# Loading one batch of queries in rows of two tokens, with the list of jobs ordered anew

## The chip, the cores and the metric

The kernel runs on one core of one Trainium2 chip. The metric is device time in microseconds (us): before the change the median of three runs is 262.52 us (262.32 to 262.54). A core has five engines that work side by side and wait for each other through semaphores: TensorE (PE, with the loading of its weights shown as PEld), VectorE (DVE), ScalarE (ACT), GpSimd (POOL) and SyncE (SP), which here only issues transfers. ACT issues a few transfers too.

## The reference, cut to what matters

Two blocks follow each other. The first is a linear attention over polynomial features; the second is a mixture of four attention experts, of which each token takes two.

```
def phi(x):                                  # 64 features of each token
    a = einsum('rd,bhsd->bhsr', S1, x); b = einsum('rd,bhsd->bhsr', S2, x)
    return einsum('bhsi,bhsj->bhsij', a, b).reshape(..., 64)
kv, z = einsum('bhsf,bhsd->bhfd', phi(k), v), sum(phi(k), over s)
x = (phi(q) @ kv) / (phi(q) @ z + 1e-6)      # (4, 4, 1088, 32) -> (4, 1088, 128)

logits = x @ w_gate;  the two best of 4 experts for each token, with softmax weights w
for e in range(4):
    a = softmax(causal((x @ wq[e]) @ (x @ wk[e]).T / 8))
    out += w_e * (a @ (x @ wv[e]) @ wo[e])   # only for tokens that chose e
```

Batch 4, heads 4, sequence 1088, head size 32, model size 128, all in float32.

## The kernel before, in words

The kernel is a list of 1284 small **jobs** (class `Plan`, L73). A job has a name, the engines it may run on, what it reads and makes, and a function that emits its instructions. `ORDER` (L21) is a list of job numbers, found ahead of time; a letter behind a number picks the first or second of the engines that the job may use. The program emits the jobs in that order. Each engine then works through its own jobs strictly in the order of the list, and waits where an input isn't there. So the list fixes the order on PE, DVE, ACT, POOL and SP, and also which of the four PSUM buffers ("pair0" to "pair3") a job gets.

Work goes by batch, and each batch in two halves. `prepare` (L423) computes x of the first block and the choice of experts; `queries`, `scores` and `values`/`outputs` (L1059 to L1324) do the experts' attention in 17 tiles of 64 tokens, in three groups (tiles 0 to 5, 6 to 11, 12 to 16). The preparation of batch b+1 lies between the attention jobs of batch b. Batch 0 has nothing in front of it; its preparation is the start-up of the kernel and uses a path of its own (`early`):

- `load k0` (L428), `load q0` (L435, `by_head`, four transfers of one head each, two issued by SP and two by ACT), `load v0` (L439, four transfers on SP). k's rows in memory are 2 KB and more, v's about 1 KB. For q, partition 32h + t holds tokens t, t + 32, t + 64 and so on of head h: each piece that a transfer moves is one token, 32 numbers or 128 bytes.
- `turn k`, `turn q` (DVE, L484 and L494) transpose 32x32 blocks, `project` (PE, L562) multiplies by both sketches at once, `low` (copy, L570) and `lift` (L574) add the high and low part, `multiply` (L580) forms the 64 features. For k they are multiply k0.0, k0.1, k0+.0, k0+.1; for q multiply q0.0 and q0+.0, .1, .2.
- `spread v0`, `spread v1` (L451) put v into place; `sums 0.0`, `sums 0.1` (PE, L619) form kv and z.
- `turn qf` (PE, L666) transposes q's features in four pieces of 6, 4, 4 and 4 blocks of 128; `keep qf` (L668) copies them out of PSUM; `numer` (L692), `divide` (L699 to L701) and `turn x` (L707) give x and its transpose, `keep x` copies that.
- `logits` (L884), `turn logits` (L888), `choose a`/`choose b` (L911 to L927) choose the experts. `store masks` and `fetch masks` (L990, L1003) send the choices through memory to all partitions; `query` (L1066), `base` and `pick` (L1079) form each token's queries for its two experts; `score` (L1104), `take` (L1116), `exp` (L1132), `guard`, `invert`, `weigh` (L1147), `turn A` (L1152), `sum` (L1180), `out` (L1251, L1277, L1301) follow.

`turn w0` to `turn w2` (L390) transpose the experts' weights, `dummy` jobs (L250) are matmuls on zeros that nobody reads. L193 is the line of a copy helper that many jobs share. Jobs of features and joins for batches 1 to 3 (`features`, L537) run mostly on POOL.

Tokens stand in their natural order from the features on. In q's path the order comes from the load:

```
eng.dma_start(out=dst[32 * h : 32 * h + 32, 0:S].rearrange("p (c d) -> p c d", d=D),
              in_=src[b, h].rearrange("(c t) d -> t c d", t=32))
```

Column block c of partition t is token 32c + t, so after a 32x32 transpose the columns are tokens in order.

Of the kernel before, what the change touches and what calls it, by code (L numbers as in the profile page):

```python
# [21 lines left out]
0 1 2 3 4 78 79 83 15a 80 45 21a 48 46 10a 81 90 53b 52b 91 54b 50 25b 18a 49 55b 5b 12a 14a 51 82 84 87 85 86 94 64  # L22
63 95b 96 27a 57 56 58 92 99 93 98b 100a 65 104 97a 101 400 89b 66a 108 103a 88a 105a 114 68 69 106 102b 70 109a 401
115 71a 110 116a 117a 107a 113a 402 399 118 124 111a 112a 59 60 120 61 406 119a 410 125a 122 405 121a 126 67 403 409
127 413 123a 414 128 408 415 134 129a 130 62 407 135 154 131 72 74 73 75 417a 419a 132 155 77 133a 136 404 137a 412
160 161 418a 140 187 138 162 163 156 158 170 188 76 157 693 192a 159 171 175 47 164 165a 176 692 191a 416a 166 189
167a 178 190 691 145 421 177 420 193 141 694 194 411 195 196 197 179 216 230 209 217 182 172 701 422a 183 218 231 198a
424 423 425 428a 223 139 219a 202 173 232 210 233a 427b 184 199 220 174a 221 180 426b 211 702 429 224 203 234 253 222
212b 254 213 185 258a 326 41b 257a 181 431 144 39b 225 255 204 235 186a 256 153 28b 236 430 200 214 226b 215 432 327
149 143 330a 331a 259 205a 142 227 329 700 438 228 168 260 433 148 332 201 328 268 698 229 206 169a 276 434 275 24b  # L30
439 207 283 699 333 277 284 208 269 261 435a 278 270 300 299 285 262 286 436a 287a 237 440 696 279b 442a 437 301 238
9b 705 695 280 441a 288 263 443 264a 708 706 302 152 281 239 303b 240a 271b 241a 289 242a 272 444 709a 282 265 304 245
244 445a 290 704 359 358 712a 273 351 446a 274 350 305 306 707a 266 147 243a 292 710a 366 713a 360 291 367 26b 267 352
361 293 369 362a 11b 353 342 343 38b 294 711a 987 246 697 151 368 363 370 464 295a 296 297 344 345 714 715 371 298 465
447 466 30b 33b 716b 146 354b 467 985 469 364 307 308 247 346b 450 309 310 717 372a 373 718 355 703 311 19b 721a 374
365 448 722b 988 470 312 719 375 468 316a 313b 720b 315b 335 314a 317 480 334 479 474 318 356 475 336 357 320 319 471
723 483a 481 337 484a 476 482 347 449 724 338b 485 486 339 451 348 340 322 321 508 725 509 487 323 548 472 501 349 488
547 324a 515 341 502 516 993 726 732 510 489 545 986 494 727 546 503 495 376 496 150 490b 477 478a 517 511a 994 733
377 995 728 518a 491 991 378 549a 504a 512 379 454 380 730b 492 729b 734 493 550b 497a 551 519 989 731 452 522 381 552
736b 382 735a 383 737 513 455 384 505 498 523 453 592 514 388a 591 385b 506 499 250 386a 249 996 524 463 461 525b 387a  # L40
593 560 526 390 248 16b 389 500 992 594 251a 738 527 595a 568 520 561 325 521 507 567 740a 391 739a 528 569 570 576
392 562 575 571b 596 563a 553 999 473 577 554 597 1002 564 462 758 621 555 458 572 759 620 1000 619 618 760 556b 578
990 573 529 579a 623a 761 530 531 534a 557 622b 558 598 624 583 1001a 580 625 584 559 393 585 651 459 532b 763 535a
1005a 1003a 764 565 581 457 533a 650 1004a 762 536 537 586 574 394 659 582 566 1007a 587a 652 658 539 643 634 538 653
635 660 661 588 589 662 642 1006a 774 773 398 460 778a 777a 590 627 644 636 645 654b 456 663 626 664b 646a 637 655 765
628 665 779 776 666 775 629 768 1008 780 1009 599 741 1010a 667 1012 630a 769 997 631 743 396 647 656 638a 600 632 657
1016a 1011 31b 601 252 639 602 633 603 742 604 1013 541 648 608a 606a 998 607b 640 605b 609 1015b 610 542 816 540 611
1014a 649 612 543a 817 795 809 766 745 641 744 810 811 770 796 812b 1017 668 771 1019 1026 544 669 670 1027 671 788
1018 749 672 748 797 1020 798a 818 673 674 751 819a 789 675 676 781 1021 678a 679a 772a 1028 1022 820 1023a 1024b 813
799 790 1025 756 1029b 1030a 814 682 782 815 791b 677a 615 681 614 680b 821 783 792 800 839 840 842 793 802 841 1031  # L50
683 843a 844a 845 613 803 1032 794 846 804 616a 757 805a 806 877 878 684 869 870 1034b 784b 912 1033a 913 755 807 746
747 917a 822 879 871 880 801 785 1052 767 1053 861 916a 786 787 872 862 808 886 1054 873b 918 885 874 881b 887 854 855
888 847 856 915 848 882 875 914 1055 889a 876 857b 883 858 849 617 13b 863 1057 823 850a 884 824 919 890 859 851 891
864 852 825 860 395 829b 826a 685 830 827b 865a 828a 944 936 1056 831 1062 686 945 921 892 920 1063 833 937 946 832
397 953 947 948b 853 922 1139 1138 952 866 1142a 867 938 955 949 1058 954 956 1143a 834 32b 1060 1140 1141 836 939 835
# [1335 lines left out]
```

## Time and profile before

| | |
|---|---|
| median of the runs shown | 262.52 us |
| the profiled execution's own time | 263.49 us |
| its span, first to last instruction | 261.8 us |
| PE busy | 254.9 us (97%) |
| DVE busy | 208.4 us (80%) |
| POOL busy | 157.5 us (60%) |
| ACT busy | 105.6 us (40%) |
| granted TensorE clock | 0.999 |

The span is what the profile's times count from; 1.7 us of the profiled execution lie around it. "Busy" for PE is an upper bound, since matmuls are pipelined and their ends are modelled. In a row of the timeline the first number is the start, the second the duration, both in us; "x" counts the instructions merged into the row, and square brackets tell how long the engine idled before and what released it. In the chain of waits the two numbers are start and length.

### The profile page before, as it was taken

How to read it: one execution, taken by the hardware profiler on the slowest of the kernel's cores; microseconds unless marked ns; L12 is line 12 of the kernel's file. 1: busy time of each engine (PE TensorE's matmuls, PEld its weight loads, DVE VectorE, ACT ScalarE, POOL GpSimd, SP SyncE). 2: the span in 40 equal slices, each digit the busy share in tenths (PEclk: the TensorE clock that was granted, in tenths of full speed). 3: DMA queues.
4: the chain of work that ended last, by engine and by line, in shares of the span. 5: the costliest groups of instructions: out<-in, count | busy, mean ns of one | idle time of the engine just before them, and what ended most of it. 6: DMA issues, size and time to landing. Idle time of an engine off the chain costs nothing.

```text
span 261.8 us, 9228 instructions
## 1 busy us (share of the span) xinstructions
PE 254.9 (97%) x3811; PEld 192.2 (73%) x3811; DVE 208.4 (80%) x529; ACT 105.6 (40%) x279; POOL 157.5 (60%) x266
## 2 busy tenths in 40 slices
PE   7899999999999999999999999999999999999995
PEld 2787666646958887665897986666689875589994
DVE  5778999999998996998887497998994388893442
ACT  3453354757242225532814044635514215723120
POOL 5546776899578716597467682366273842542642
PEclk9999999999999999999999999999999999999999
DMA  7978689891467275906044685003370379240012
GB/s 149 212 122 186 112 207 168 158 146 20 73 135 166 67 184 114 148 4 183 3 84 83 143 167 120 4 3 90 93 120 4 96 141 238 47 96 3 5 30 59
DMA packets 87739, 27.35 MB, mean 104 GB/s; under 512 B 58576, under 2 KB 87056, under 8 KB 87696
## 3 DMA queue, kind: packets, MB, share of 16 engines
q1 hardware_dynamic: 85184, 26.15, 50.7%
q10 hardware_dynamic: 2512, 0.61, 1.0%
q8 instruction: 30, 0.49, 0.8%
q14 instruction: 13, 0.11, 0.2%
HBM read 22.22 MB, written 4.52 MB: 102 GB/s over the span
## 4 chain that ended last, share of the span: by engine, by line
PE 84%; DMA 8%; DVE 5%; POOL 1%; issue 1%; SPq 0%; ACT 0%; DVEq 0%; POOLq 0%; ACTq 0%
PE pair L1180 28%; PE pair L1104 24%; PE pair L1066 9%; PE pair L1301 7%; DMA mb<-md 4%; PE pair L1251 3%; PE pair L523 2%; PE pair L827 2%; DMA in<-in_q_dram 2%; DMA w<-in_v_dram 2%; PE pair L627 2%; DVE w L1116 1%; PE pair L1277 1%; DVE fp L805 1%; PE pair L619 1%; PE pair L692 1%
## 5 line engine op out<-in xcount | busy, mean ns | idle before, releaser
L1147 POOL TENSOR_SCALAR w<-w,rs,sh 128x256 f32<-128x256 f32 (+14 forms) x68 | 56.8, 840 | 34.4 <-DVE rs L1143 32.8
L1104 PE MATMUL pair<-xT,qs 128*128 128x320 f32 (+9 forms) x216 | 74.0, 478 | 0.4 <-DVE qs L1079 0.4
L1132 ACT ACTIVATE w<-w,mx 128x64 f32<-128x64 f32 (+15 forms) x68 | 52.4, 772 | 45.8 <-DVE mx L1116 40.6
L1116 DVE CUSTOM_DVE_ANT_0 w<-pair,mask 128x64 f32<-128x64 f32 (+14 forms) x68 | 48.3, 723 | 15.4 <-PE pair L1104 13.0
L1104 PEld LDWEIGHTS pair<-xT,qs 128*128 128x128 f32 x216 | 38.8, 190 | 25.9 <-issue 11.1
L1152 DVE STREAM_TRANSPOSE AT<-w 128x320 f32<-128x320 f32 (+15 forms) x68 | 51.2, 762 | 3.4 <-POOL w L1147 3.0
L1180 PEld LDWEIGHTS pair<-AT,xra 32*128 32x128 f32 x1136 | 41.6, 185 | 4.6 <-issue 2.0
L1180 PE MATMUL pair<-AT,xra 32*128 32x160 f32 (+5 forms) x1136 | 44.9, 303 | 0.0
L1207 POOL TENSOR_TENSOR agg<-agg,mb 128x768 f32<-128x768 f32 (+1 forms) x22 | 34.0, 1559 | 3.4 <-DVE agg L1203 2.0
L1066 PE MATMUL pair<-xT,Mq 128*128 128x384 f32 (+1 forms) x96 | 34.0, 475 | 0.0
L193 ACT COPY agg<-pair 128x384 f32<-128x384 f32 (+1 forms) x31 | 13.2, 463 | 45.5 <-PE pair L1180 44.0
L1180 PEld LDWEIGHTS pair<-AT,xrb 32*128 32x128 f32 x752 | 26.4, 185 | 2.4 <-issue 2.2
L1180 PE MATMUL pair<-AT,xrb 32*128 32x160 f32 (+5 forms) x752 | 28.0, 289 | 0.0
L1140 POOL TENSOR_SCALAR rs<-zs 128x1 f32<-128x1 f32 x32 | 6.8, 214 | 34.0 <-ACT w L1132 23.5
L1066 PEld LDWEIGHTS pair<-xT,Mq 128*128 128x128 f32 x96 | 17.3, 190 | 10.3 <-issue 3.2
L1079 DVE COPY_PREDICATED qs<-mb,pair 128x768 f32<-128x768 uint16 (+1 forms) x24 | 23.1, 962 | 1.5 <-ACT qs L193 0.3
L537 POOL TENSOR_TENSOR fp<-w 128x576 f32<-128x576 f32 x19 | 22.6, 1209 | 1.6 <-DVE w L527 1.1
L1301 PEld LDWEIGHTS pair<-Mo,agg 128*128 128x128 f32 x168 | 20.6, 192 | 2.4 <-issue 0.5
L1301 PE MATMUL pair<-Mo,agg 128*128 128x128 f32 x168 | 21.4, 277 | 0.0
L193 ACT COPY qs<-pair 128x384 f32<-128x384 f32 (+1 forms) x21 | 9.2, 463 | 19.5 <-PE pair L1066 14.2
L1203 DVE COPY_PREDICATED agg<-mb,pair 128x384 f32<-128x384 uint16 (+1 forms) x24 | 12.7, 557 | 4.8 <-ACT agg L193 4.4
L1132 ACT ACTIVATION_READ_ACCUMULATOR w<-w,mx 128x1 f32 x68 | 12.8, 189 | 0.0
(179 smaller groups left out, 297.2 us busy)
## 6 DMA issues: line engine op xcount, KB each, us to landing
xra<-xd SPq DMA_DIRECT2D x16, 192.0 KB, 5.2
xrb<-xd SPq DMA_DIRECT2D x16, 192.0 KB, 5.4
xrc<-xd SPq DMA_DIRECT2D x16, 160.0 KB, 5.0
mb<-md SPq DMA_DIRECT2D x4, 576.0 KB, 7.4
mb<-md SPq DMA_DIRECT2D x4, 480.0 KB, 4.4
mb<-md SPq DMA_DIRECT2D x6, 288.0 KB, 4.3
in<-in_k_dram SPq DMA_DIRECT2D x12, 136.0 KB, 3.4
in<-in_q_dram SPq DMA_DIRECT2D x3, 544.0 KB, 5.6
```

What stands on the lines that cost most here:

```text
L193: (nc.scalar.copy if eng == "ACT" else VEC[eng].tensor_copy)(o, i)
L537: VEC[e].tensor_tensor(out=f, in0=a[:, :, None, R : 2 * R].to_broadcast([128, j1 - j0, R, R]), in1=a[:, :, 0:R, None].to_broadcast([128, j ...
L1066: nc.tensor.matmul(plan[ps[x]][:, y, 0:w], Mq[:, ((1, 2), (0, 3))[x][y]], plan[xT][:, 64 * t0 : 64 * t1], start=True, stop=True)
L1079: nc.vector.copy_predicated(chosen(), rows(c), rows(plan[ps[x]]))
L1104: nc.tensor.matmul(plan[p][:, y, 0 : c1 - c0], plan[qs][:, 128 * t : 128 * t + 128], plan[xT][:, c0:c1], start=True, stop=True)
L1116: nc.vector.tensor_tensor_reduce(out=o, in0=src, in1=msk, scale=-1.0, scalar=mx[:, b, i, x - 1 : x] if x else 3e38, op0=ALU.add, op1=ALU.m ...
L1132: nc.scalar.activation(out=a, in_=a, func=ACTF.Exp, bias=mx[:, b, i, last : last + 1], scale=-1.0, accum_out=zs[:, b, i : i + 1])
L1147: nc.gpsimd.tensor_scalar(out=a, in0=a, scalar1=rs[:, b, i : i + 1], scalar2=plan[("sh", b)][:, i : i + 1], op0=ALU.mult, op1=ALU.mult)
L1152: nc.vector.transpose(dst[:, 0 : keys // 32, t], plan[A][:, 0:keys].rearrange("p (j s) -> p j s", s=32))
L1180: nc.tensor.matmul(plan[Vk[g // 2]][:, g % 2, lo : 32 * nt], plan[(f"xr{j // 12}", b)][rows, j % 12], a[rows, j, lo:], start=(j == 0), sto ...
L1207: nc.gpsimd.tensor_tensor(out=a, in0=a, in1=plan[mb][:, 2 * x : 2 * x + 2, 0:w], op=ALU.mult)
L1301: nc.tensor.matmul(plan[p][0:m, 0, 128 * x : 128 * x + 128], plan[agg][:, e, 128 * x : 128 * x + m], Mo[:, e], start=(e == 0), stop=(e == ...
```

## The change

Four jobs load batch 0's q in rows of two neighbouring tokens (64 numbers, 256 bytes), with half as many rows. Column block 2c + x of partition t is now token 64c + 2t + x. After the transposes the columns of each stretch of 64 tokens stand with the even tokens first and the odd ones behind. Features are formed per token, so they do not mind; `keep_features` writes them back to their natural place, with a step of two elements in the destination. Its first piece (6 blocks, in two PSUM banks) becomes two copies of 384 columns in place of one of 768; the other three stay one copy of 512 columns.

```
+        def by_pairs(eng, dst, src, h):
+            eng.dma_start(out=dst[32 * h : 32 * h + 32, 0:S].rearrange("p (c y) -> p c y", y=2 * D),
+                          in_=src[b, h].rearrange("(c t x) d -> t c (x d)", t=32, x=2))
...
-                job(f"load q{b}.{x}", ("SP", "ACT")[x % 2], 0.7, lambda e, x=x: by_head(nc.scalar if e == "ACT" else nc.sync, plan[qin], q, x),
+                job(f"load q{b}.{x}", ("SP", "ACT")[x % 2], 0.7, lambda e, x=x: by_pairs(nc.scalar if e == "ACT" else nc.sync, plan[qin], q, x),
...
         def keep_features(e, y0, y1, t):
-            if y1 - y0 > 4:
-                w = 64 * (y1 - y0)
-                copy(e, plan[qpT][:, 128 * y0 : 128 * y1].rearrange("p (a y) -> p a y", a=2), plan[t][:, :, 0:w])
-            else:
-                copy(e, plan[qpT][:, 128 * y0 : 128 * y1], plan[t][:, 0, 0 : 128 * (y1 - y0)])
+            w = (y1 - y0) // (2 if y1 - y0 > 4 else 1)
+            for a in range((y1 - y0) // w):
+                o = plan[qpT][:, 128 * (y0 + w * a) : 128 * (y0 + w * a + w)].rearrange("p (m t x) -> p m x t", t=32, x=2)
+                copy(e, o, plan[t][:, a, 0 : 128 * w].rearrange("p (m x t) -> p m x t", t=32, x=2))
```

`ORDER` is replaced as a whole. It holds the same 1284 jobs, and the same PE jobs with the same work (seven dummies as before). 95 jobs change engine, 10 of them dummies, most of the others single copies and `guard`s. The start-up, engine by engine (written out from the two lists):

```
        before                                         after
PE      project k0, dummy, project k0+, repeat S2,     project k0, repeat S2, dummy, project k0+,
        project q0, q0+, sums 0.0,                     project q0, q0+, turn w2, sums 0.0,
        turn w0, w1, w2, sums 0.1,                     turn w1, w0, sums 0.1,
        turn qf 0.0, .3, .1, .2, numer 0.0,            turn qf 0.0, .2, .1, .3, numer 0.0,
        sketch k1, turn x 0.0, numer 0.2, 0.1,         sketch k1, turn x 0.0, numer 0.2, 0.1,
        logits 0.0, products, turn x 0.1, 0.2,         logits 0.0, products, turn x 0.1, 0.2,
        query 0.0.00, logits 0.1, 0.2,                 query 0.0.00, query 0.0.01, logits 0.1, 0.2,
        query 0.0.01, widen 1, 0, ...                  widen 0, 1, ...
DVE     turn k0.0, k0.1, spread3, low k0, lift k0,     turn k0.0, diagonal0, turn k0.1, spread3, low k0, lift k0,
        turn q0.0, q0.1, multiply k0.0, lift k0+,      turn q0.0, q0.1, multiply k0.1, lift k0+,
        multiply k0+.1, lift q0, lift q0+,             multiply k0+.1, lift q0+, lift q0,
        multiply q0.0, q0+.2, .0, .1                   multiply q0.0, q0+.1, .0, .2
ACT     low k0+, keep S2, spread v0, low q0, low q0+,  keep S2, low k0+, spread v0, low q0+, low q0,
        keep w, keep sums, keep qf                     keep w, keep sums, keep qf
POOL    multiply k0.1, spread v1, multiply k0+.0       multiply k0.0, spread v1, multiply k0+.0
SP      v0.0, v0.3, v0.1, v0.2, w1, w0, w2,            v0.3, v0.0, v0.1, v0.2, w2, w0, w1,
        k1, w3, w4                                     k1, w4, w3
```

Behind the start-up, scores, queries, sums and outputs of the same batches stand in nearly the same coarse order, shuffled among neighbours. PE's jobs have "modes" by how they use the array: the whole 128 rows (query, score, out, transposes), or parts of it (sums, sketches, numer, logits). In the list before, PE goes from a part mode to the whole 33 times, 22 of these from `numer 1` on; in the new list 29 times, 20 of these from `numer 1` on.

Between the last query of a group and the first score that needs it, the new list has on PE: behind the queries of group 2 of batch 1 `out 0.2` and half of `score 1.10`; behind those of group 2 of batch 2 `out 1.2`; behind those of group 1 of batch 2 `numer 3`. The list before had at these places, in turn, three sum jobs, `score 1.10` and `out 0.2`; three sum jobs and `out 1.2`; `out 1.1.0` and `numer 3`.

More of the change, by code (lines that the diff above doesn't have):

```diff
@@ L27 @@
[L27 to L31, printed above, removed]
@@ L52 @@
[L52 to L55, printed above, removed]
-868 950 923 951 940b 928 35b 837a 924a 838 957 754 750 22b 929 753 1144 941 752 1145 1168 942 930 958b 1169 1185 959
@@ L70 @@
+1282 1130 42b 1131 1281 1132b 1280 1134b 1283 1133a 1136a 1137b 1135a
 """.split()
```

87 lines of the change are left out of this document (48 added, 39 removed).

## The prediction

> **What bounds the kernel now.** The page's first lines come first, then the chain of waits, then PE's own waits.
>
> ```profile
> span 261.8 us, 9228 instructions
> PE 254.9 (97%) x3811; PEld 192.2 (73%) x3811; DVE 208.4 (80%) x529; ACT 105.6 (40%) x279; POOL 157.5 (60%) x266
> ```
>
> ```profile
> 1.87 4.53 DMA in<-in_q_dram
> ...
> 6.42 4.52 DMA w<-in_v_dram
> ...
> 11.09 1.84 POOL vp L193
> ...
> 12.97 1.12 PE pair L619 x32
> 14.09 0.81 PE pair L390 x6
> 14.90 1.29 PE pair L619 x40
> 16.19 2.11 PE pair L666 x18
> ...
> 33.12 9.43 DMA mb<-md
> ...
> 54.53 8.06 PE pair L1104 x22
> ...
> 255.88 2.69 PE pair L1277 x24
> ```
>
> ```profile
> PE pair L619 <- POOL vp L193: 0.9, 1, 0.9
> PE pair L1104 <- DVE qs L1079: 0.4, 1, 0.4
> PE pair L827 <- DVE w L527: 0.3, 1, 0.3
> ```
>
> See three stretches. Up to 12.97 the chain runs through data: q's load, then v's, then POOL's spread of v, for which PE waited 0.9 us. From 23 to 52 PE's pieces alternate with DVE's and with the mask transfer (33.12 to 42.55). From 54.53 to the end there is nothing but PE, and PE's list of waits holds no other wait behind its first 7 us. The PE jobs stay the same, so the time can fall by an earlier start of the packed stretch or by less loss between PE's own jobs; it rises by every wait that the new list opens. The diff's first stretch reaches PE only through v, since q's own use stands behind `lift k0` on DVE and starts there without a wait (no bracket):
>
> ```profile
> 8.66 1.37 DVE L494 STREAM_TRANSPOSE in<-in 128x384 f32<-128x384 f32 x2
> ```
>
> **The rows of q.** Packets of four stretches: 6.3 to 6.7 (only q, both queues), 10.5 to 11 (only weights, rows of 256 bytes, one queue), 13 to 13.5 (only rows of 128 bytes, one queue), 3.6 to 4.2 (mostly k, rows of 2 KB, both queues).
>
> ```profile
> DMA packets 681, 0.09 MB, mean 215 GB/s; under 512 B 681, under 2 KB 681, under 8 KB 681
> ```
>
> ```profile
> DMA packets 438, 0.11 MB, mean 217 GB/s; under 512 B 438, under 2 KB 438, under 8 KB 438
> ```
>
> ```profile
> DMA packets 711, 0.09 MB, mean 181 GB/s; under 512 B 711, under 2 KB 711, under 8 KB 711
> ```
>
> ```profile
> DMA packets 108, 0.21 MB, mean 344 GB/s; under 512 B 13, under 2 KB 13, under 8 KB 108
> ```
>
> Half the rows does not mean half the time: 128-byte rows already move 215 GB/s on two queues, 256-byte rows 217 on one. q is 0.557 MB, so 2.6 us at 215. The ends: 217 GB/s (nothing gained) and 344 (1.6 us, 1.0 gained). I take the step that one queue shows, 181 to 217, a fifth: 215 x 1.2 = 258 GB/s, 2.2 us, 0.4 gained. v, behind q on SP's queue, lands at 10.5 instead of 10.94.
>
> The Trainium skill, "DMA: Bandwidth & Descriptors", Specifications, wants at least 512 bytes for line rate, with a read-modify-write below; by that rule 256-byte rows stay slow and nothing is gained, which is the second rival below. The same page, "Why small descriptors are slow", gives about three extra cycles per packet beside one per 32 bytes; as an estimate that is 11 cycles for 256 bytes against twice 7, a fifth less, near the value taken.
>
> **The start-up behind v.** DVE and POOL from 8 to 18 us, and ACT's copies of the features:
>
> ```profile
> 11.05 0.96 DVE L580 TENSOR_TENSOR fp<-w 128x768 f32<-128x768 f32 x1
> ```
>
> ```profile
> 12.65 0.56 DVE L574 TENSOR_TENSOR w<-pair,w 128x384 f32<-128x384 f32 x1 [0.30 <-ACT w L193]
> 13.13 1.75 DVE L580 TENSOR_TENSOR fp<-w 128x768 f32<-128x768 f32 x1
> ```
>
> ```profile
> 11.09 1.83 POOL L193 COPY vp<-w 64x1024 f32<-64x1024 f32 x1 [1.22 <-DMA w<-in_v_dram]
> 12.99 1.07 POOL L580 TENSOR_TENSOR fp<-w 128x512 f32<-128x512 f32 x1
> ...
> 17.84 1.46 POOL L378 CAST AT<-ident 64x1536 bf16<-64x1536 f32 x1
> ```
>
> ```profile
> 9.83 2.27 PE L562 MATMUL pair<-SD,in 128*128 128x128 f32 x18
> ```
>
> See that DVE's multiply and POOL's instruction hold each other up: the multiply at 13.13 takes 1.75 us beside POOL's multiply, 0.96 at 11.05; and POOL's spread, begun 0.04 behind the multiply at 11.05, takes 1.83, where a cast of 1536 columns takes 1.46, so 1024 should take 1.0. With v at 10.5 the spread starts at 10.6, ahead of that multiply, and ends at 11.6. The multiply (k0+.1) follows, 11.6 to 12.55, then POOL's k0+.0, to 13.65.
>
> PE: `project q0+` ends at 12.1 as before. One weight turn moves ahead of `sums 0.0` (0.81 / 3 = 0.27): sums 0.0 runs from 12.4 to 13.5, the other two turns to 14.05, sums 0.1 to 15.35, `turn qf` (2.11) to 17.45, against 18.30: **0.85 earlier**. q's features keep up: the second lift (0.5 to the next start) now comes first, the smaller one behind it ends about 13.5, the multiply waits for POOL until 13.65, and at the 0.96 for 768 columns the four end near 14.6, 15.2, 15.9 and 16.5, ahead of the last four transposes at 17.0. If v came no earlier, only the moved weight turn is gained: 0.3. At best all of PE's wait goes, 1.15.
>
> **The copies that restore the order.** ACT's rows, and the `numer` that needs all four:
>
> ```profile
> 17.03 2.27 ACT L193 COPY fp<-pair 128x768 f32<-128x768 f32 x4 [0.36 <-PE pair L666]
> ```
>
> ```profile
> L193 ACT COPY fp<-pair 128x768 f32<-128x768 f32 x1 | 0.8, 799 | 0.4 <-PE pair L666 0.4
> ```
>
> ```profile
> L193 ACT COPY agg<-pair 128x384 f32<-128x384 f32 (+1 forms) x31 | 13.2, 463 | 45.5 <-PE pair L1180 44.0
> ```
>
> ```profile
> 21.09 1.63 PE L692 MATMUL pair<-kvz,fp 128*64 128x66 f32 x48
> ```
>
> Two copies of 0.46 replace one of 0.80, +0.13. They start at 16.2 and end at 18.6; `numer 0.2` wants them at 20.25 (21.09 - 0.85), so 1.65 us of cover. No row shows a destination with steps of two: ends are no cost and double time (2.4 more, which outlasts the cover by 0.75). I take no cost, by the rows of equal width.
>
> The Trainium skill, "SBUF — State Buffer", Door 1, has lines of 16 bytes that run at full rate with two hits per line; a step of two float32 values gives exactly two, so by that rule the copies cost nothing more. No run here shows it yet.
>
> **The choice of experts.** PE and DVE around 25 us:
>
> ```profile
> 25.05 0.81 PE L1066 MATMUL pair<-xT,Mq 128*128 128x384 f32 x2
> 25.79 0.80 PE L884 MATMUL pair<-xT,wg 128*32 128x192 f32 x16
> ```
>
> ```profile
> 25.21 0.65 PE pair L1066 x2
> ```
>
> ```profile
> 26.74 0.56 DVE L888 STREAM_TRANSPOSE ch<-pair 128x192 f32<-128x192 f32 x2
> ```
>
> In the new list a second query (0.65) goes ahead of `logits 0.1` and `0.2`. Before, DVE took them at 26.74 without idling; now it idles about 0.5 there, and behind it on DVE stand the second choice, `store masks`' input and the picks of group 0, for which PE already waited 0.4. So of 0.85 some 0.35 are left along DVE, the mask transfer (33.12 to 42.55) and PE's wait on L827. Ends: 0 (the transfer doesn't move) and 0.85 (DVE catches up, idle elsewhere).
>
> **PE's changes of mode.** A single score between two sums:
>
> ```profile
> 195.12 1.05 PE pair L1104 x2
> ```
>
> It is score 3.7, 512 columns. At the query's rate (384 columns in 0.65) it should take 0.87, so an entry into the whole array costs about 0.2. In the packed stretch the list has 20 entries instead of 22: **0.4 less**. The two saved earlier lie where DVE decides; ends 0 and 0.8.
>
> **The sum.** 0.35 + 0.4 = 0.75: span 261.8 becomes 261.05. The profiled execution took 263.49, 1.7 around its span; the median runs stand 0.7 above the span. I take the difference on the median: 262.52 - 0.75 = **261.8 us**.
>
> **Rivals.** *The whole start-up arrives*: DVE is late at 26.7 for other reasons and the extra query costs nothing, 0.85, and all four entries count, 0.8: 260.9. For it: DVE's row at 26.74 has no bracket, so it came late for reasons of its own. Against it: those are settled by then, and the logits come 0.65 later.
>
> *The rows do not do what they say*: 256 bytes move at 217 GB/s, v lands at 10.94, POOL loses again. Then 0.3 is gained at turn qf, 0.5 lost at the logits, 0.4 won on modes: 262.3. For it: 215 and 217 GB/s; against it: 344.
>
> *Slower: the picks come late.* The list places less PE work between a group's last query and its first score.
>
> ```profile
> L1079 DVE COPY_PREDICATED qs<-mb,pair x24: 820/998/1040, 30.1 to 224.0; 128x768 f32<-128x768 uint16 x16, 128x640 f32<-128x640 uint16 x8
> ```
>
> ```profile
> 226.09 2.21 PE pair L1251 x8
> ```
>
> ```profile
> L1152 DVE STREAM_TRANSPOSE AT<-w 128x320 f32<-128x320 f32 (+15 forms) x68 | 51.2, 762 | 3.4 <-POOL w L1147 3.0
> ...
> L1203 DVE COPY_PREDICATED agg<-mb,pair 128x384 f32<-128x384 uint16 (+1 forms) x24 | 12.7, 557 | 4.8 <-ACT agg L193 4.4
> ```
>
> Behind the queries of batch 2's and batch 1's last groups PE has one `out` of 2.21 us left, where it had three sums more. DVE must pass there two patches or kept sums (0.5 each), one turn (0.76), the pick (0.82 and more) and maybe half of the pick before it: 2.7 to 3.2, a wait of 0.5 to 1.0 each; behind `numer 3` a like wait of 0.5 is possible. Together up to 2.5, at the middle about 1.7, for 262.52 - 0.75 + 1.7 = 263.5. It decides from 0.95 us of such waits on, that is, where two of the three places bite. Against it: the list before showed 0.4 of such waits in all.
>
> **How the numbers follow.** Forecast 0.42 (own range 261.3 to 262.2), whole start-up 0.15, rows without effect 0.15, late picks 0.28. Less than 0.2% (0.5 us) can't be told from no change, so faster means below 262.0. Two thirds of the forecast and the first rival: 0.44; same: the rest of the forecast and most of the second rival, 0.26; slower: the picks and a little of the second, 0.30. The range goes from 260.6 (1.15 at the start-up and 0.8 on modes) to 263.8 (late picks with 2.0 of the 2.5).
>
> **What the new profile would show.** q's stretch well above 215 GB/s, v's spread near 10.6 and 1.0 long, sums at 12.4, turn qf ended near 17.5; the first copy in two pieces, total about 2.4; DVE idle about 0.5 ahead of the later logits; the masks landed near 42.2; PE's waits on L1079 still near 0.4. I am wrong if v lands as before, if the stepped copies take double, or if PE's wait list grows entries behind 54 us.

## The result: 0.5% slower, and the profile after

The changed kernel takes 263.97 us (median of 12 runs, 263.21 to 265.53), the kernel before beside it 262.62 (12 runs, 262.19 to 264.26). The ratio is **1.0054 [1.003, 1.0078]**: about 1.35 us slower. The forecast was 261.8 with a range up to 263.8; sign and range both missed.

First the page of the changed kernel, then its chain of waits (start, length in us), then PE's own waits in full.

```profile
span 262.2 us, 9226 instructions
PE 254.4 (97%) x3811; PEld 192.0 (73%) x3811; DVE 207.9 (79%) x536; ACT 105.9 (40%) x285; POOL 154.0 (59%) x254
```

```profile
15.60 2.11 PE pair L670 x18
...
52.01 2.16 PE pair L830 x43
54.17 8.06 PE pair L1107 x22
...
212.23 7.96 DMA mb<-md
222.84 2.47 PE pair L1107 x6
...
255.98 2.69 PE pair L1280 x24
```

```profile
PE pair L1107 <- DVE qs L1082: 1.4, 2, 0.9
PE pair L250 <- DVE idle L243: 1.3, 1, 1.3
PE pair L566 <- DVE in L488: 0.9, 1, 0.9
PE pair L830 <- DVE w L531: 0.4, 1, 0.4
```

See three things. `turn qf` (L670) ends at 17.71 against 18.30, and the packed stretch starts at 54.17 against 54.53, 0.36 sooner, as the forecast had it (0.35). In that stretch, where PE waited for nothing before, stands a mask transfer of 7.96 us, and PE's wait for the picks (L1082, which was L1079) has grown from 0.4 to 1.4 us. And PE's wait for v is gone. By the spans (261.8 and 262.2) the kernel is 0.4 slower, by the medians 1.35: the profile of before came from an execution that took 263.49 us, 0.97 above the median of its first three runs and 0.87 above that of the twelve. So the first experiment is a second profile of before.

### The profile page after: what moved, and what is told of

It is laid out like the page before. It is cut to its first block, busy times and chain, and to the rows that moved or that the text cites. A ratio compares the mean times of both kernels' runs of the same rounds, so it can differ in the third digit from the quotient of the medians.

```text
span 262.2 us, 9226 instructions
## 1 busy us (share of the span) xinstructions
PE 254.4 (97%) x3811; PEld 192.0 (73%) x3811; DVE 207.9 (79%) x536; ACT 105.9 (40%) x285; POOL 154.0 (59%) x254
## 4 chain that ended last, share of the span: by engine, by line
PE 86%; DMA 6%; DVE 3%; ACT 1%; POOL 1%; issue 1%; SPq 1%; ACTq 0%; DVEq 0%
PE pair L1183 28%; PE pair L1107 23%; PE pair L1069 10%; PE pair L1304 6%; PE pair L1254 3%; DMA mb<-md 3%; PE pair L527 3%; PE pair L830 2%; PE pair L566 2%; PE pair L631 2%; DMA in<-in_k_dram 1%; DMA vp<-in_v_dram 1%; DVE qs L1082 1%; PE pair L1280 1%; PE pair L623 1%; PE pair L695 1%
## 5 line engine op out<-in xcount | busy, mean ns | idle before, releaser
L1150 POOL TENSOR_SCALAR w<-w,rs,sh 128x64 f32<-128x64 f32 (+16 forms) x68 | 56.0, 828 | 44.3 <-DVE rs L1146 41.2
L1135 ACT ACTIVATE w<-w,mx 128x768 f32<-128x768 f32 (+15 forms) x68 | 52.5, 772 | 69.8 <-DVE mx L1119 64.2
L1107 PE MATMUL pair<-xT,qs 128*128 128x384 f32 (+11 forms) x216 | 73.2, 478 | 1.4 <-DVE qs L1082 1.4
L1119 DVE CUSTOM_DVE_ANT_0 w<-pair,mask 128x768 f32<-128x768 f32 (+14 forms) x68 | 48.5, 724 | 16.1 <-PE pair L1107 14.8
L1107 PEld LDWEIGHTS pair<-xT,qs 128*128 128x128 f32 x216 | 38.6, 190 | 27.2 <-issue 11.6
L1155 DVE STREAM_TRANSPOSE AT<-w 128x384 f32<-128x384 f32 (+15 forms) x68 | 50.4, 757 | 4.6 <-POOL w L1150 4.5
L1183 PE MATMUL pair<-AT,xra 32*128 32x160 f32 (+5 forms) x1136 | 44.1, 303 | 0.0
L1210 POOL TENSOR_TENSOR agg<-agg,mb 128x768 f32<-128x768 f32 (+1 forms) x22 | 34.1, 1558 | 12.4 <-ACT agg L193 7.6
L1082 DVE COPY_PREDICATED qs<-mb,pair 128x768 f32<-128x768 uint16 (+1 forms) x24 | 23.1, 961 | 5.6 <-ACT qs L193 2.5
L541 POOL TENSOR_TENSOR fp<-w 128x576 f32<-128x576 f32 x20 | 23.6, 1202 | 1.4 <-DVE w L531 1.3
L1304 PE MATMUL pair<-Mo,agg 128*128 128x128 f32 x168 | 20.4, 277 | 0.0
L1143 POOL TENSOR_SCALAR rs<-zs 128x1 f32<-128x1 f32 x28 | 6.0, 212 | 16.6 <-ACT w L1135 12.4
L193 DVE COPY agg<-pair 128x384 f32<-128x384 f32 (+1 forms) x13 | 6.8, 530 | 7.4 <-PE pair L1183 5.4
```

What stands on the lines that cost most here:

```text
L193: (nc.scalar.copy if eng == "ACT" else VEC[eng].tensor_copy)(o, i)
L541: VEC[e].tensor_tensor(out=f, in0=a[:, :, None, R : 2 * R].to_broadcast([128, j1 - j0, R, R]), in1=a[:, :, 0:R, None].to_broadcast([128, j ...
L1082: nc.vector.copy_predicated(chosen(), rows(c), rows(plan[ps[x]]))
L1107: nc.tensor.matmul(plan[p][:, y, 0 : c1 - c0], plan[qs][:, 128 * t : 128 * t + 128], plan[xT][:, c0:c1], start=True, stop=True)
L1119: nc.vector.tensor_tensor_reduce(out=o, in0=src, in1=msk, scale=-1.0, scalar=mx[:, b, i, x - 1 : x] if x else 3e38, op0=ALU.add, op1=ALU.m ...
L1135: nc.scalar.activation(out=a, in_=a, func=ACTF.Exp, bias=mx[:, b, i, last : last + 1], scale=-1.0, accum_out=zs[:, b, i : i + 1])
```

## Experiments

A kernel's time varies by 2 to 3 us from run to run; in the profiles nearly all of the difference is made before 54 us. So three numbers of the one profiled execution are set beside the median: where PE's sums of batch 0 start, the packed stretch from its start near 54 us (L1104 or L1107) to the end of PE's last matmul (L1277 or L1280) and the tail from there to the end of the span. For after they come from the chain above: 255.98 + 2.69 - 54.17 = 204.50, and 262.2 - 258.67 = 3.53; for the others from the same rows.

| kernel | median us | ratio to before | sums start | packed stretch | tail |
|---|---|---|---|---|---|
| before | 262.62 | | 12.97 | 204.04 | 3.23 |
| after | 263.97 | 1.0054 [1.003, 1.0078] | 12.51 | 204.50 | 3.53 |
| e1 before again | 262.63 | 0.9977 [0.9958, 0.9996] | 11.72 | 204.17 | 3.24 |
| e2 rows only | 263.46 | 0.9996 [0.9976, 1.0016] | 12.41 | 204.02 | 3.25 |
| e3 list only | 263.65 | 1.0029 [1.0002, 1.0056] | 12.17 | 203.95 | 3.52 |
| e4 after, four masks | 263.47 | 1.0016 [0.9996, 1.0037] | 12.68 | 203.40 | 3.62 |
| e7 whole rows, old list | 263.49 | 1.0019 [0.9992, 1.0046] | 12.58 | 204.03 | 3.23 |
| e8 list, four masks | 263.2 | 1.0005 [0.9982, 1.0029] | 12.26 | 203.42 | 3.44 |
| e9 e8 and store order | 263.09 | 1.0011 [0.9984, 1.0037] | 12.10 | 203.41 | 3.46 |
| e10 after, three on SP | 264.43 | 1.0052 [1.0026, 1.0077] | 12.79 | 203.40 | 3.49 |
| e11 after again | 264.0 | 1.0041 [1.0019, 1.0063] | 12.27 | 204.13 | 3.54 |
| e12 all mended | 263.61 | 1.0024 [1.0002, 1.0046] | 13.64 | 203.41 | 3.46 |
| e13 gap filled | 263.35 | 1.0013 [0.9993, 1.0032] | 13.48 | 203.42 | 3.60 |
| e15 query back | 262.86 | 0.9988 [0.9968, 1.0008] | 12.71 | 203.41 | 3.53 |
| e16 rows, gap filled | 263.9 | 1.0022 [0.9997, 1.0046] | 12.68 | 203.39 | 3.51 |
| e17 rows, query back | 262.83 | 0.9995 [0.9976, 1.0014] | 12.56 | 203.41 | 3.52 |
| e18 query back again | 262.82 | 0.9974 [0.9959, 0.9989] | 12.06 | 203.42 | 3.52 |

Before's kernel ran again beside each block of experiments, with medians of 263.15 (e1 to e4), 262.92 (e5 to e8), 262.88 (e9 to e12), 263.22 (e13 to e16) and 263.53 (e17, e18); the ratios are to these. All 169 executions of its code on record, e1's among them, have a median of 262.98; 54 took 263.49 or more, 27 took 262.39 or less.

Theories at the outset: the *list* costs (its late mask, and more), the rows are harmless; the *rows* cost (q and v land later); and the rival on record, picks that come late by DVE's own work.

### e1: before once more

No edit.

> The kernel before, unchanged, for a typical profile of it: the one shown stands about 1 us above its own median, the changed kernel's does not. All theories expect 262.3 to 262.7 us, the same as before within 0.2%. The list theory (the new list opens a wait for the mask transfer of batch 3 near 210 us) expects this profile, held against the changed kernel's, to be level or some 0.3 us late at 54 us, and to win about 1 us or more from 205 us on. The rows theory (q in rows of 256 bytes lands its last piece and v later) expects it to be ahead already at 54 us.

The identical code measured 0.9977 of itself, with an interval that leaves out 1. So a ratio of 0.2 to 0.3% is not settled by one interval here. The packed stretch is the better witness: it lies between 204.02 and 204.17 in all four profiles with the old list in the table. The start of its chain:

```profile
6.19 4.28 DMA w<-in_v_dram
...
10.61 1.06 POOL vp L193
11.72 1.12 PE pair L619 x32
```

v's last transfer is issued at 6.19 (6.42 in the first profile of before), POOL's spread gets ahead of DVE's multiply and takes 1.06 instead of 1.84 us, and PE's sums start 1.25 us sooner, without the wait for POOL. From there on the two profiles run side by side. The list theory had expected e1 level with the changed kernel at 54 us, the rows theory ahead: it reaches 53.29, 0.88 us ahead of 54.17. But e1's profile is no more typical than the first. It comes from an execution of 262.39 us, one of the fastest sixth, and the first from one of the slowest third. As an estimate from the stretches (1.7 around the span, tail 3.2, packed stretch 204.1), an execution of before that takes 262.98 us reaches the packed stretch at 54.0, one of 262.62 at 53.6. So the changed kernel, whose profile stands at its median, is 0.2 to 0.5 us late there, and the 0.36 that it seemed to win was won against a slow start.

### e2, e3, e4: the change in parts

```
e2:  the new load and keep_features, with ORDER of before
e3:  before's code, with the new ORDER
e4:  the changed kernel, and
-        "mb": several("mb", 3, [128, 6, GW], BF16),
+        "mb": several("mb", 4, [128, 6, GW], BF16),
```

> q in rows of two tokens and the copies that restore the order, with the list of before. List theory: the rows change nothing that reaches the end, 262.4 to 262.9 us, since PE's stream behind 54 us follows the old list. Rows theory: q's last piece and v land some 0.3 to 0.5 us later, nothing hides it at the start, 263.0 to 263.9 us, with PE's sums of batch 0 starting later than 12.97 and the turn of q's features ending later than 18.3.

> The old rows of one token with the new list. List theory: as slow as the changed kernel, 263.5 to 264.3 us, with the pick of batch 3, group 0 waiting for its mask near 220 us. Rows theory: the list gains about 0.5 us and the rows took it back, 261.9 to 262.3 us. Rival that was on record (picks late by DVE's own work, not by the mask): 263.5 to 264.3 us as well, but with PE's waits on the picks spread over groups 1 and 2 of batch 2 and group 2 of batch 1.

> The changed kernel with four mask buffers instead of three, so that the fetch for batch 3, group 0 needn't wait until POOL has spread the values of batch 2, group 2 (209 to 212 us). List theory with the mask as its cause: the fetch is issued several us earlier, DVE's wait of 2.25 us at 220 us goes, PE's waits on the picks fall from 1.4 to about 0.4 us, and the time falls by 0.6 to 1.0 us to 263.0 to 263.4. If the picks are late by DVE's own work, or the rows cost: 263.7 to 264.2, no change. If the later mask only shifts the next wait: a gain under 0.3.

e2 came out at 263.46, 0.8 above e1 but only 0.3 above the 35 runs of before on the same chip (ratio 0.9996, not told from no change); e3 at 263.65, 1.0 and 0.5 above (1.0029). So the rows by themselves are not shown to cost anything here, and the list has only part of the loss. e2's packed stretch is that of before, so rows act only at the start. e3 and e4 show the list's part. Around 220 us, the changed kernel and then e4 (DVE's picks):

```profile
212.51 1.87 DVE L1082 COPY_PREDICATED qs<-mb,pair 128x640 f32<-128x640 uint16 x2 [0.49 <-ACT qs L193]
220.31 1.01 DVE L1082 COPY_PREDICATED qs<-mb,pair 128x768 f32<-128x768 uint16 x1 [2.25 <-DMA mb<-md]
```

```profile
213.31 1.87 DVE L1082 COPY_PREDICATED qs<-mb,pair 128x640 f32<-128x640 uint16 x2 [0.49 <-ACT qs L193]
219.22 1.03 DVE L1082 COPY_PREDICATED qs<-mb,pair 128x768 f32<-128x768 uint16 x1 [0.36 <-ACT qs L193]
```

And the issues of the masks on SP around it, again after, then e4:

```profile
208.44 0.41 SPq L860 DMA_DIRECT2D xrc<-xd  x1
212.23 0.38 SPq L1002 DMA_DIRECT2D mb<-md  x1
```

```profile
209.23 0.41 SPq L860 DMA_DIRECT2D xrc<-xd  x1
209.69 0.46 SPq L1002 DMA_DIRECT2D mb<-md  x1
```

With three buffers the fetch for batch 3, group 0 must wait until POOL has spread the last values of batch 2, group 2 (the multiply with the mask on L1210); SP issues nothing from 208.85 to 212.23. POOL's last two such multiplies in after, 2.77 us together, end at 212.2:

```profile
209.44 2.77 POOL L1210 TENSOR_TENSOR agg<-agg,mb 128x640 f32<-128x640 f32 x2 [4.96 <-ACT agg L193]
```

The transfer takes 8 us. Before issues the same fetch no sooner, at 212.89, but its first pick that needs the mask comes only at 222.94; in after it comes at 220.31, wait and all. Before's two picks of batch 3, group 0:

```profile
222.94 2.13 DVE L1079 COPY_PREDICATED qs<-mb,pair 128x768 f32<-128x768 uint16 x2
```

DVE works in the order of the list, so in after it stands for 2.25 us, and PE behind it for 0.56:

```profile
219.96 0.86 PE L1107 MATMUL pair<-xT,qs 128*128 128x416 f32 x2
221.38 0.81 PE L1107 MATMUL pair<-xT,qs 128*128 128x320 f32 x2 [0.56 <-DVE qs L1082]
```

In e4 the fetch is issued 2.5 us sooner (209.69 against 212.23), though e4 as a whole runs 0.8 later there; it no longer ends the wait, and the packed stretch falls to 203.40. It is 203.39 to 203.42 in all ten kernels of the table that have the new list without that wait, and 203.95 to 204.50 in the three profiles that have it. So the wait costs 0.55 to 1.1 us, and the list without it gains 0.65 on before. e4's median fell by 0.5 only; its profile lost 0.7 again at 52 us (below).

### e5, e6, e7: what the rows do

```
e5:  ORDER of before, with load v0.0 to v0.3 and load w0 to w2 moved behind
     load k1.1, ahead of spread v1
e6:  the same with the new load and keep_features
e7:  before, with one row for each partition, order of tokens not restored:
+    eng.dma_start(out=dst[32 * h : 32 * h + 32, 0:S],
+                  in_=src[b, h].rearrange("(t c) d -> t (c d)", c=C))
```

> For the landing of q alone: the list of before with the transfers of v and of three weights moved behind those of k of batch 1, which wait for PE, so that after k only q's rows of one token are on the way (v and all behind it come late; the time itself means nothing). In the kernel before, with v behind it, q's last piece landed 5.6 us after its issue. Theory that v overtakes: q's four pieces land here about as there, 5.2 to 5.6 us at most, at about 215 GB/s and 1700 packets per us. Theory that bytes alone bound: the same.

> The same with q in rows of two tokens. With v behind it q's last piece, the second of ACT's queue, landed 6.5 to 6.7 us after its issue, a us later than with rows of one token. Theory that v overtakes (SP's half of q is done sooner, v's packets of 1 KB then share the engines with ACT's half): alone, the four pieces land together, the last at 4.7 to 5.1 us, sooner than with rows of one token, and the stretch moves 250 GB/s or more. Theory that bytes alone bound: 5.2 to 5.6, at 215 GB/s. Theory that a row of 256 bytes is by itself slower or unevenly spread: 6 us or more although nothing is behind it.

> The kernel before with q of batch 0 in one row of 4352 bytes for each partition (34 tokens, as k's rows are), order of tokens not restored (so batch 0's output belongs to other tokens; the work is the same). It asks what the start is worth if q's transfer is as fast as it can be. If q's packets are what v waits for: q lands a us or more sooner, v too, PE's sums start near 11.2 instead of 11.7 to 13.0, and the time falls by 0.5 to 1 us below before, 261.7 to 262.2. If q's transfer isn't what sets v's landing, or PE then waits for DVE and POOL: no change, 262.4 to 263.2.

Stretches of 5 to 5.5 and 6.5 to 7 us in e5 (6 to 6.5 is as the first), 5 to 5.5, 6 to 6.5 and 6.5 to 7 us in e6, and q's landings (two transfers each; last number: median us from issue to landing):

```profile
DMA packets 854, 0.11 MB, mean 216 GB/s; under 512 B 854, under 2 KB 854, under 8 KB 854
...
DMA packets 803, 0.10 MB, mean 202 GB/s; under 512 B 803, under 2 KB 803, under 8 KB 803
...
in<-in_q_dram SPq DMA_DIRECT2D x2, 136.0 KB, 5.0
in<-in_q_dram ACTq DMA_DIRECT2D x2, 136.0 KB, 5.2
```

```profile
DMA packets 559, 0.14 MB, mean 285 GB/s; under 512 B 557, under 2 KB 557, under 8 KB 559
DMA packets 369, 0.09 MB, mean 184 GB/s; under 512 B 369, under 2 KB 369, under 8 KB 369
DMA packets 297, 0.07 MB, mean 145 GB/s; under 512 B 297, under 2 KB 297, under 8 KB 297
...
in<-in_q_dram SPq DMA_DIRECT2D x2, 136.0 KB, 4.9
in<-in_q_dram ACTq DMA_DIRECT2D x2, 136.0 KB, 5.3
```

(e5 took 270.93 and e6 271.46 us, one run each; v comes late in both, so the times say nothing of the rows.) Rows of 128 bytes hold 216 GB/s, and 202 in the last half us. Rows of 256 bytes move 285 at first, faster than I had forecast, and fall to 145 while q is still on its way; from 5 to 7 us as a whole it is 212 and 213 GB/s, and the last piece lands as late as before. Neither theory of the two had this: a fast start and a long end, as if some of the 16 engines were done and others not (the trace doesn't split a stretch by engine, so that is an inference). e7 goes to the far end: rows of 4352 bytes land 5.4 us (SP's two, median) and 5.9 us (ACT's two) after their issue, no sooner, and PE's sums start at 12.58. **Larger rows of q don't bring the start forward.** (In e7 q was there when DVE turned it at 9.18; DVE was late by its work on k.) With v behind it, the long end is what v meets, as I read it; the turn of q and the spread of v in after:

```profile
9.18 1.37 DVE L498 STREAM_TRANSPOSE in<-in 128x384 f32<-128x384 f32 x2 [0.64 <-DMA in<-in_q_dram]
...
11.41 1.05 POOL L193 COPY vp<-w 64x1024 f32<-64x1024 f32 x1 [1.73 <-DMA w<-in_v_dram]
```

With the old rows DVE turned q at 8.66 (before), 8.33 (e1), 8.73 (e8) and, after a wait of 0.39, 8.79 (e3); with rows of two tokens at 9.18 (after), 9.45 (e2), 9.44 (e4) and 8.84 (e11), each time waiting for q: about 0.6 later. e13, with the old rows, turned q at 9.18 too, but without a wait, behind a late k.

### e8 and e9: the list without its mask wait, and the tail

```
e8:  e3 with four mask buffers
e9:  e8, and at the end of ORDER
-1137b 1135a
+1135a 1137b
```

> The old rows with the new list and four mask buffers: the list without its mask wait and without the rows. If both are what the change lost, this is the best so far: stretch from 54 us to the last output 203.4 us (204.1 in before), start as in before, 0.3 us lost again at the tail: 262.0 to 262.5, level with before or 0.3 us better. If the new list loses elsewhere too (before 54 us, or by a lower granted clock): 262.8 to 263.5.

> Old rows, new list, four mask buffers, and the last two stores issued in the order of the list before (store out 3.0.1 on SP ahead of 3.0.2 on ACT). If that order is what makes the tail longer (3.25 us from PE's last matmul to the end of the span in before, 3.46 to 3.64 with the new list): tail 3.25, and this would be the best version: span near 260.5, 262.0 to 262.6. If the tail stays at 3.5, its length comes from the copies or the transfers: 262.4 to 262.9. If the start with the new list is slower by its clock: above 263.

e8's profile is the forecast one (stretch 203.42, 262.63 us for that execution), but its median is 263.2. The order of the last two stores isn't what lengthens the tail: 3.46 in e9. The new list's tail is 3.44 to 3.62 in every profile that can be read so, the old list's 3.23 to 3.25; its cause stays open. It lies behind the last issue: from the issue of ACT's last store the span has 2.86 us left in before (2.88 in e1), 3.16 in after and 3.10 in e9.

e9's profile took 264.32 us, and shows something else: PE's granted clock (columns: stretch, its length, PE's busy time and instructions, clock, DMA share, GB/s).

```profile
32.00:34.00 2.00, 2.00 (x24) 1.00 0.51 130
34.00:37.50 3.50, 3.50 (x38) 0.53 0.78 211
37.50:40.00 2.50, 2.50 (x55) 0.98 1.15 277
```

The same stretches in e8, whose kernel differs only in the order of the two stores:

```profile
32.00:34.00 2.00, 2.00 (x24) 1.00 0.57 152
34.00:37.50 3.50, 3.50 (x75) 1.00 0.83 216
```

For about 3.4 us TensorE runs at half its clock, and gets through 38 matmuls instead of 75. `numer 1` starts at 53.47 instead of 51.78: 1.7 us lost. The dip begins at 34.2; 2.4 us ahead of it ends PE's only wait nearby, 0.89 us before the first score; e8 and after have the same gap:

```profile
31.82 1.25 PE L1099 MATMUL pair<-xT,qs 128*128 128x64 f32 x6 [0.89 <-DVE qs L1074]
```

With the old list the gap is 0.38 (before) and 0.27 (e1). Each run lists a clock. Below 0.996 it was in 18 of 96 runs of the kernels with this gap (after, e3, e4, e8 to e12), among them 4 of the 12 of after, at 0.994 and 264.88 to 265.53 us; with the old list in none of 181 runs that list one.

### e10, e11, e12: v behind q, and everything mended

```
e10: the changed kernel, and (with load q0.3 ahead of load v0.3 in ORDER)
-    job(f"load q{b}.{x}", ("SP", "ACT")[x % 2], 0.7, ...
+    job(f"load q{b}.{x}", ("SP", "ACT", "SP", "SP")[x], 0.7, ...
e11: the changed kernel
e12: e10 with four mask buffers and e9's order of stores
```

> The changed kernel with three heads of q on SP's queue and one on ACT's, so that v, behind SP's three, can't pass a piece of q on ACT's. Theory that v overtakes: q's last piece lands by 8.3 us instead of 9.1 to 9.3, DVE's turn of q starts at 8.3 to 8.8 without the wait of 0.4 to 1.1, PE's sums start 0.3 to 0.7 sooner (near 12.0): 263.2 to 263.7. If q is late for another reason, or POOL's spread of v decides in any case: 263.7 to 264.2, no change.

> The changed kernel itself, beside its mended versions in one place, and for a second profile of it: 263.7 to 264.2; PE's sums from 12.4 to 12.7, DVE's wait for q, the wait for the mask near 220 us (0.5 us at PE or more) and a tail of 3.5 should all come again. If the wait for the mask does not come again, it was chance.

> The changed kernel with all three mended: three heads of q on SP's queue, four mask buffers, the last stores in the old order. If the three losses are what made it slower, they add up to 0.4 (start), 0.8 (mask) and 0.25 (tail): 262.4 to 262.9, level with before. If rows or list lose somewhere else: 263.2 or more.

The theory that v overtakes q isn't borne out: with three heads on SP's queue q is turned at 9.32, still waiting for it, and v is spread later, not sooner (ACT's part at 11.36 instead of 10.92); 264.43. e10's packed stretch was 203.40 although it has three buffers: its mask fetch was issued at 212.86, later than after's, yet the pick at 219.05 waits for ACT alone, so the transfer landed in under 6.2 us where after's took 7.96 and e11's 7.61. The mask wait thus depends on the execution too: at 8 us the fetch is late, at 6 it is not. e11 repeats the change (264.0), its mask wait (1.9 us at DVE, stretch 204.13) and its tail. e12's profile has a late start (sums at 13.64, PE having waited 0.73 for POOL's spread of v); its 263.61 is 0.8 below e10 and still above before (1.0024).

### e13 to e16: the gap at 31 us

```
e13: e9 with dummy12 and dummy36 run behind sums 1.1 (17b, 41b become 17a, 41a)
e14: e8 with sums 1.0 and 1.1 behind score 0.2.00 instead of ahead of score 0.0.00
e15: e9 with query 0.0.01 behind logits 0.2 instead of ahead of logits 0.1
e16: e13 with the new load and keep_features
```

> Old rows, new list, four mask buffers, and two of the matmuls on zeros (dummy12 and dummy36), which the new list skips, run behind sums 1.1, where PE idles 0.89 us before the first score. If that gap is what brings TensorE's half clock: none of 12 runs below 0.996 (about 2 of 12 without), PE's wait at 31 us near 0, time as the better runs of e9, 262.3 to 262.9. If the gap isn't the cause: about 2 of 12 below 0.996.

> Old rows, new list, four mask buffers, with the sums of batch 1 (2.29 us of PE) moved from ahead of the first scores to behind them, so that PE idles 3.2 us instead of 0.89 at 28.6 to 31.8. If an idle gap there brings the half clock: nearly all of 12 runs below 0.996, half clock for 3 us or more from about 32 us, and the time 1 to 2 us longer, 264 to 265.5. If the gap isn't the cause: clock as in e8 (1 of 12 below 0.996), and the time 0 to 0.7 longer, since DVE sets the pace until 52 us.

> Old rows, new list, four mask buffers, with the query that the new list puts ahead of logits 0.1 and 0.2 moved back behind them. If it is what makes the gap: DVE's idle 0.3 at 26.2 goes, the picks come 0.3 to 0.65 sooner, PE's wait at 31 us falls from 0.89 to 0.2 to 0.6 and the clock stays above 0.996 in all 12 runs; time 262.2 to 262.8. If the gap has another maker: PE's wait unchanged at 0.9.

> As e13 with the rows of two tokens: the changed kernel with four mask buffers and the gap filled. Held against e13 it tells what the rows alone are worth, in one place: if v and q land 0.2 to 0.5 later with them, 0.2 to 0.5 us above e13; if rows make no difference, level with it.

Widening the gap settles that idle time there can bring the half clock, if it is long. e14, 269.57 us, all of its 6 runs at 0.980 to 0.985:

```profile
28.00:30.00 2.00, 0.74 (x3) 1.00 0.73 140
30.00:32.00 2.00, 0.17 (x2) 1.00 0.66 117
32.00:34.00 2.00, 2.00 (x8) 0.50 0.57 152
34.00:42.00 8.00, 7.66 (x94) 0.50 1.08 216
```

Ten us at half clock follow a gap of 3.1. e5 and e6 agree: 4.0 and 3.9 us of PE idling for v, then about 10 us at 0.50 (to 25.8 and 25.3). e15 tells what makes the gap in the new list: with the query back behind the later logits DVE no longer idles at 26 us (0.29 in after), and PE's score starts without a wait:

```profile
PE pair L245 <- DVE idle L238: 1.3, 1, 1.3
PE pair L614 <- POOL vp L188: 0.8, 1, 0.8
PE pair L822 <- DVE w L522: 0.5, 1, 0.5
```

None of e15's 12 runs has a low clock. Filling the gap with matmuls on zeros did not do as much: the wait is gone in e13's and e16's profiles, yet 5 of their 24 runs are still below 0.996 (1 and 4, one of these 270.36 us at 0.948), the same share as with the gap. Why, the profiles don't show, since both had a full clock. So that the gap of 0.89 brings the short dips is likely, by e14 and e15, but not shown: e13 and e16, which close the gap with less change to the list, speak against it.

### e17 and e18: rows and no rows in the mended list

e18 is e15 again, e17 the same with the new load and keep_features.

> The changed kernel (rows of two tokens) with four mask buffers, the last stores in the old order and the query back behind the later logits. If PE's gap at 31 us was the only maker of the half clock: no run of 12 below 0.996. If the rows cost 0.3 to 0.5 us, as e13 against e16 and e1 against e2 had it: 0.3 to 0.5 us above e18; if they cost nothing: level with it.

> e15 once more (old rows, new list, four mask buffers, last stores as before, query back), for a second interval: 262.5 to 263.0, the stretch from 54 us on 203.38 again, no run of 12 below 0.996. If 0.7 us from the later stretch are gained and 0.3 lost at the tail, it is 0.3 to 0.5 us faster than before; if the start with the new list is later by as much, level with it.

1 of 12 and 0 of 12 with a low clock; with e15 1 of 36 for the list with the query back, against 18 of 96. e17 and e18 have the same median (262.83, 262.82), though e18's fastest is 0.33 below e17's. What rows of two tokens cost, by the ratios to before: -0.0004 (e2), 0.0012 (e11 against e3), 0.0011 (e4, e8), 0.0009 (e16, e13) and 0.0021 (e17, e18). Each is within its intervals; together they say no gain, and a cost of about 0.3 us at the middle (0 to 0.55). e18 is the fastest version (old rows, new list, four mask buffers, query back): 0.9974 [0.9959, 0.9989], and the identical e15 0.9988. By the stretches it gains 204.10 - 203.42 = 0.68 and loses 0.28 at the tail. But before itself, as e1, measured 0.9977: that e18 is faster than before is not shown by its time.

## Why the prediction was wrong, point by point

- **From the profile to the median (fails).** On the two profiles the start came as forecast, 0.36 for 0.35. The step that fails is "I take the difference on the median": the 0.85 at `turn qf` is counted from an execution in which PE waits 0.86 for POOL's spread of v, and is then taken off a median that lies 0.97 below that execution's time. The wait comes and goes with the execution: e1, the same kernel, has none and ends `turn qf` at 17.05, 0.66 ahead of after's 17.71; e15 has 0.8 and e18, the same kernel again, none. Held against an execution of before at its median, the changed kernel is 0.2 to 0.5 late at 54 us, by the estimate under e1. The step should have asked what an execution nearly 1 us above the median spends it on.
- **The rows of q (fails).** Forecast 258 GB/s and v landed at 10.5; the stretch of 6.3 to 6.7 us moved 215 before and 218 after, with less than half the packets:

```profile
DMA packets 308, 0.09 MB, mean 218 GB/s; under 512 B 295, under 2 KB 308, under 8 KB 308
```

  v's spread starts at 11.41, not 10.6, later than the 11.09 of before. `turn qf` still ended 0.59 sooner on the two profiles, by luck and not by an earlier v: DVE had waited for q and came to its multiply at 11.56 instead of 11.05, so that POOL's spread got ahead of it all the same. The rival "rows without effect" was nearer, yet too kind: DVE's turn of q comes about 0.6 us later. The hold-up between POOL and DVE is as described: v's spread, now first, takes 1.05, and the multiply beside it 1.71.

```profile
11.56 1.71 DVE L584 TENSOR_TENSOR fp<-w 128x768 f32<-128x768 f32 x1
```

- **The copies (right, size off).** They cost neither nothing nor double. After, then e18, whose copies are the old ones:

```profile
L193 ACT COPY fp<-pair 128x512 f32<-128x512 f32 x3 | 1.7, 676 | 0.0
L193 ACT COPY fp<-pair 128x384 f32<-128x384 f32 x2 | 0.9, 520 | 0.4 <-PE pair L670 0.4
```

```profile
L188 ACT COPY fp<-pair 128x512 f32<-128x512 f32 x3 | 1.6, 604 | 0.0
L188 ACT COPY fp<-pair 128x768 f32<-128x768 f32 x1 | 0.8, 799 | 0.4 <-PE pair L661 0.4
```

  A copy of 512 columns takes 0.07 more. The four copies overlap at their ends, so the row as a whole counts: 2.27 us before, 2.51 now,

```profile
16.45 2.51 ACT L193 COPY fp<-pair 128x384 f32<-128x384 f32 x5 [0.37 <-PE pair L670]
```

  0.24 more where I had 0.13, all of it under the cover of 1.65. By the Trainium skill, "SBUF — State Buffer", Door 1, two accesses to a line of 16 bytes are enough for full bandwidth, and a step of two float32 gives two. The trace does not bear that out: 12% more (653 ns in e2, 8%). Whether the step or the finer pattern of the copy costs it, no run separates.
- **The choice of experts (right in place, wrong in price).** DVE idles 0.29 ahead of the later logits where I had 0.5, and 0.36 was left at 54 us. What I missed is the other side of it: PE's gap before the first score goes from 0.38 to 0.89, and in a fifth of the runs with it the clock is low; after's four take 1.1 to 1.7 us more than the median of its others. The Trainium skill, "TensorE: Matmul & The Clock Gate", Part 1, has a free-running window of about 3.4 us and half rate after an idle one. The length of e9's dip (3.4 us) and its chance nature agree with that; that a whole idle window is needed is not borne out: ahead of the dip stood 3.08 us of idling in e14's profile (and all its 6 runs have a low clock), 0.89 in e9's.
- **The modes (right, undersized).** 0.4 forecast; the packed stretch without the mask wait is 0.65 shorter. That is the whole difference of the two lists there; that the two entries make it was not tried alone.
- **The late picks (fails: right sign, wrong cause).** The sum has nothing for a new wait in the packed stretch, and the sign to look for was "PE's waits on L1079 still near 0.4". I had the rival at 263.5 with three places, all by DVE's own work. The wait came at a fourth, for the mask transfer of batch 3: I counted DVE's and PE's jobs between a query and its score, but not when the buffer of the mask comes free, nor that the fetch takes 8 us. It costs 0.55 to 1.1, and turns the 0.4 forecast for this stretch into 0.46 lost (204.04 to 204.50).
- **The tail** (0.3) was in no step.

On the two profiles, then, the span rose by 0.40: 0.36 won at the start, 0.46 lost in the packed stretch and 0.30 at the tail, where 0.35, 0.4 and 0 were to be won. The medians add that before's profile stood 0.87 above its median, and after's 0.05.

Seen from the medians, and as estimates: the list's packed stretch is about 0.2 longer than before with its mask wait (204.32, mean of after and e11, against 204.10), the tail 0.3, the rows about 0.3 (0 to 0.55), the half clock 0.2 of the median (without those four runs it is 263.8). That is 1.0, where the first twelve runs of each show 1.35, and all 169 of before against the 24 of after and e11 (263.99) show 1.0. What the rows lose may in part be lost at 52 to 55 us: `numer 1`, 2.18 us of PE in after, takes 2.78 to 3.1 in e2, e4, e11 and e16, with PE waiting for nothing that the profile shows. That is four of the nine profiles with rows of two tokens and none of the eleven others (2.5 and 2.6 in e1 and e7); whether the rows have to do with it stays open.

## What to carry to other kernels

Before counting a wait as something to be won, see whether the profiled execution stands at the kernel's median; start-up waits on transfers can be that execution's luck. One more profile can be just as far off on the other side. When a list is ordered anew, follow for every wait on a transfer the buffer that lets it start and the time that it takes, not the engines' jobs alone. On a matmul-bound kernel a wait on PE may cost more than its length, because the clock may halve behind it (shown here for a wait of 3.1 us, likely for 0.9); look at the clock of every run, not at the profiled one's.

## What the runs showed of the hardware

- Transfers of 128 and of 256 bytes a row moved the same over q's 5 to 7 us, 212 and 213 GB/s (e5, e6), though the second began at 285 and ended at 145; rows of 4352 bytes landed no sooner (e7).
- PE gaps of 3.1 us (e14, all 6 runs), 3.9 and 4.0 us (e6, e5, one run each) were followed by about 10 us at half clock. A gap of 0.89 us was followed in e9, 2.4 us after its end, by 3.4 us at half clock; 18 of 96 runs with such a gap had a low clock, but so had 5 of 24 with the gap filled by matmuls on zeros.
- An ACT copy of 512 columns out of PSUM with steps of two float32 at its destination took 653 to 676 ns (e2, after) against 604 to 605 without (e18, before): 8 to 12% longer.
